# Chunked attention and a multiplicative feed-forward: another order of steps, with 100 zero products at its head

## The chip, the cores and the metric

The kernel runs on one core of one Trainium2 chip. The time is the device time of one execution in microseconds (us). A core has five engines that run side by side, each with its own queue in order: TensorE (PE, matrix products), VectorE (DVE), ScalarE (ACT), GpSimd (POOL) and SyncE (SP). PE writes its products to PSUM, a small memory of 8 banks; the other engines take them from there. POOL and SP also start DMA transfers, which 16 DMA engines carry out. An engine waits for another by semaphores.

## The reference

Attention within chunks of 64 positions, then a feed-forward whose two branches are multiplied:

```python
B, H, S, D = 8, 8, 576, 64;  chunk = 64
scores = scale * np.matmul(q_c, k_c.transpose(0, 1, 2, 4, 3))
attn = softmax(scores)                      # over the 64 positions of the chunk
x = np.matmul(attn, v_c)                    # gathered to (4608 tokens, 512)
a = x @ w1;  b = x @ w2                     # 512 -> 1024 each
out = ((a * b) @ w3) @ w_out                # 1024 -> 1024 -> 512
```

q, k, v and the weights are float32 in device memory. The kernel works in bfloat16 with float32 sums, and multiplies w3 by w_out once ahead (w3o), so the last two products are one.

## The kernel before, in words

The 72 chunks are worked in 18 *pairs* p = 0 to 17, each of 4 chunks (256 tokens). Every piece of work is a *step* with a letter and a pair, and the text `ORDER` (lines 9 to 40) lists all steps in the order in which they are issued. Nothing is planned at run time: each engine works its own share of that list in order. The letters:

- `q`, `k`, `v`: loads of a pair, started by POOL; `i0` to `i3`: quarters of w1 and w2; `o`: w_out; `h0`, `h1`: halves of w3. `R0`, `R1`: raw loads of pair 0's q and k on SP and ACT, which `K` casts. At most 8 of POOL's loads are under way: each waits for the landing of the eighth before it. There are 5 buffers for q and k (a pair each) and 6 for v.
- `T p.s`: DVE transposes q or k (line 205; 1.3 us). `G`: from pair 6 on, 8 moves on SP bring two pairs' transposed q and k into a form with fewer matmuls (line 216). `S`: scores on PE (line 226: 64 matmuls for pairs 0 to 5, 32 for later ones); `E`: exponential on ACT; `P`: product with v on PE (again 64 or 32 matmuls).
- `N p.u`: DVE divides by the sums (lines 266, 269); `X`: DVE transposes the result for the feed-forward; `H`: moves of it on SP for pairs from 6 on.
- `A`, `B`: products with w1 and w2 on PE (line 344); pairs 0 to 3 alone with 256 columns, later ones in twos with 512. `C`: ACT copies A's product from PSUM (line 367); `M`: DVE multiplies it by B's (line 384).
- `V`, `W`, `Z`: w3 times w_out: 8 transposes on DVE (line 425), 4 groups of 16 matmuls, 4 casts on ACT. V0 to V3 need `h0`, V4 to V7 `h1`; the two halves of a W need one V each.
- `O`: the last product (16 matmuls of 512 columns), `Y`: ACT copies it out of PSUM, `Q`: SP stores it.
- `D which.p.j.n.cols`: n matmuls of a zero tile into a PSUM tile, cols wide; their result is overwritten (lines 323 to 329).
- `x p`: POOL copies one element of pair p's attention result, so that the loads behind it wait for that (line 164).

PSUM holds 4 tiles of 2 banks. The lines that matter below: a matmul is always issued through one helper (line 96), as a weight load and a product, so each is two instructions of PE's program. That program is one straight list of 5,323 instructions.

Of the kernel before, what the change touches and what calls it, by code (L numbers as in the profile page):

```python
# [7 lines left out]

ORDER = """
R0 R1 v0 q1 k1 i0 v1 i1 i2 q2 k2 v2 i3 q3 k3 v3 q4 k4 v4 o h0 h1 D0.0.0.16.64 K0 T0.0 K1 T0.1 q5 k5  # L10
v5 S0 T1.0 E0 P0 D0.1.0.4.512 T1.1 q6 k6 v6 N0.0 S1 D1.0.0.5.512 X0.0 N0.1 X0.1 A0.0 E1 B0.0 C0.0 P1
M0.0 A0.1 N1.0 X1.0 B0.1 C0.1 N1.1 A0.2 X1.1 B0.2 M0.1 C0.2 A1.0 A1.1 B1.0 T2.0 T2.1 q7 B1.1 S2 M0.2
C1.0 C1.1 A0.3 E2 M1.0 P2 k7 B0.3 M1.1 A1.2 N2.0 C0.3 A1.3 B1.2 N2.1 X2.0 T3.0 C1.2 B1.3 X2.1 T3.1
C1.3 A2.0 M0.3 C2.0 B2.0 M1.2 q8 S3 A2.1 M1.3 A2.2 M2.0 E3 P3 T4.0 C2.1 C2.2 B2.1 N3.0 B2.2 N3.1
A2.3 B2.3 X3.0 X3.1 A3.0 M2.1 C2.3 M2.2 k8 A3.1 M2.3 B3.0 B3.1 T4.1 C3.0 q9 M3.0 C3.1 M3.1 A3.2 v7
V0 B3.2 C3.2 V1 A3.3 M3.2 S4 B3.3 W0 k9 C3.3 V2 V3 W1 Z0 V4 V5 T5.0 V6 V7 W2 Z1 W3 M3.3 T5.1 q10
T6.0 E4 T6.1 Z2 P4 T7.0 S5 T7.1 N4.0 Z3 k10 O0 T8.0 O1 q11 E5 N4.1 X4.0 Y0 G3.0 q12 X4.1 Y1 k11 P5
v8 N5.0 N5.1 O2 Q0 X5.0 X5.1 G3.1 A4.0 O3 T8.1 C4.0 Y2 S6 E6 S7 T9.0 T9.1 Q1 B4.0 T10.0 M4.0 A4.1
G4.0 T10.1 E7 P6 Y3 B4.1 v9 N6.0 C4.1 N6.1 A4.2 G4.1 C4.2 B4.2 M4.1 X6.0 M4.2 A4.3 P7 q13 q14 N7.0
Q2 B4.3 C4.3 A4.4 N7.1 k12 B4.4 M4.3 A4.5 X6.1 C4.4 C4.5 B4.5 A4.6 k13 k14 C4.6 M4.4 A4.7 S8 T11.0  # L20
v10 B4.6 B4.7 M4.5 q15 X7.0 X7.1 M4.6 C4.7 S9 M4.7 E8 P8 N8.0 O4 E9 N8.1 Q3 P9 Y4 H3.0 O5 T11.1 X8.0
T12.0 H3.1 v11 T12.1 Y5 N9.0 T13.0 A6.0 G5.0 B6.0 N9.1 X8.1 C6.0 X9.0 A6.1 C6.1 B6.1 T13.1 A6.2 B6.2
X9.1 M6.0 G5.1 A6.3 C6.2 H4.0 H4.1 q16 M6.1 B6.3 A6.4 M6.2 B6.4 C6.3 S10 M6.3 v12 C6.4 G6.0 E10 A6.5
T14.0 T14.1 M6.4 C6.5 B6.5 A6.6 M6.5 C6.6 B6.6 A6.7 C6.7 P10 M6.6 S11 N10.0 B6.7 A8.0 B8.0 E11 Q4
G6.1 N10.1 C8.0 M6.7 M8.0 X10.0 X10.1 k15 P11 A8.1 A8.2 B8.1 N11.0 B8.2 k16 A8.3 C8.1 C8.2 N11.1
X11.0 B8.3 A8.4 M8.1 v13 B8.4 S12 C8.3 M8.2 S13 C8.4 H5.0 X11.1 M8.3 A8.5 E12 A8.6 C8.5 M8.4 B8.5
C8.6 T15.0 H5.1 B8.6 A8.7 B8.7 T15.1 M8.5 E13 P12 M8.6 A10.0 T16.0 B10.0 N12.0 C8.7 A10.1 N12.1 M8.7
P13 C10.0 v14 M10.0 C10.1 B10.1 N13.0 N13.1 A10.2 M10.1 X12.0 A10.3 B10.2 X12.1 C10.2 C10.3 q17
A10.4 M10.2 B10.3 x12 G7.0 B10.4 X13.0 G7.1 C10.4 A10.5 v15 k17 M10.3 X13.1 M10.4 x11 A10.6 S14 S15
T16.1 T17.0 T17.1 B10.5 C10.5 B10.6 C10.6 E14 O6 M10.5 Q5 M10.6 E15 P14 N14.0 N14.1 G8.0 Y6 X14.0 O7  # L30
Y7 P15 G8.1 A10.7 H6.0 B10.7 S16 C10.7 N15.0 E16 N15.1 X14.1 X15.0 v16 v17 S17 M10.7 O8 E17 H6.1 Q6
Y8 P16 A12.0 B12.0 N16.0 A12.1 C12.0 M12.0 P17 B12.1 C12.1 N16.1 A12.2 C12.2 X15.1 B12.2 N17.0 H7.0
A12.3 C12.3 Q7 N17.1 M12.1 B12.3 A12.4 B12.4 M12.2 C12.4 A12.5 B12.5 M12.3 C12.5 M12.4 A12.6 Q8
C12.6 A12.7 H7.1 B12.6 B12.7 O9 C12.7 Y9 M12.5 M12.6 A14.0 B14.0 C14.0 M12.7 M14.0 A14.1 C14.1 A14.2
B14.1 A14.3 X16.0 C14.2 Q9 B14.2 X16.1 O10 Y10 M14.1 X17.0 H8.0 B14.3 A14.4 Q10 C14.3 X17.1 A14.5
M14.2 B14.4 C14.4 O11 Y11 A14.6 C14.5 M14.3 M14.4 A14.7 H8.1 A16.0 C14.6 B14.5 B14.6 B14.7 M14.5
C14.7 M14.6 Q11 M14.7 B16.0 A16.1 A16.2 C16.0 A16.3 B16.1 M16.0 C16.1 M16.1 A16.4 C16.2 C16.3 B16.2
C16.4 M16.2 A16.5 B16.3 O12 Y12 M16.3 C16.5 B16.4 A16.6 O13 Y13 M16.4 A16.7 B16.5 M16.5 C16.6 C16.7
Q12 B16.6 O14 B16.7 M16.6 Q13 O15 Y14 Q14 Y15 Q15 M16.7 O16 Y16 Q16 O17
"""  # L40


# [543 lines left out]
```

## Time and profile before

| | |
|---|---|
| time, median of 3 runs (all) | 245.23 us (243.93, 245.23, 246.45) |
| the profiled execution | 243.69 us, its span 242.1 us |
| PE busy | 225.9 us; last matmul ends at 238.86 us |
| DVE, ACT, POOL busy | 153.3, 84.2, 83.7 us |
| DMA engines | 0.9 busy or more until about 150 us |
| queue q8 (instructions) | 21 packets of 16,384 bytes |

The landing times that are used below, from the trace (us): the two parts of i1 18.06 and 19.17, of i2 20.52 and 21.84; k2 25.19; v2 26.51; the first half of w3 until 49.21, the second until 54.58; q5 56.01, k5 57.46; q10 80.91, k10 84.67.

A line of the timeline gives start, duration, engine, source line, operation, result and inputs, how many of them; in brackets the idle time of the engine ahead of it and what ended it ("issue": nothing that the profile shows). A line of the waits gives who waited for whom, us in total, how often, the longest. A line of the chain gives start, length and what it was.

### The profile page before, as it was taken

How to read it: one execution, taken by the hardware profiler on the slowest of the kernel's cores; microseconds unless marked ns; L12 is line 12 of the kernel's file. 1: busy time of each engine (PE TensorE's matmuls, PEld its weight loads, DVE VectorE, ACT ScalarE, POOL GpSimd, SP SyncE). 2: the span in 40 equal slices, each digit the busy share in tenths (PEclk: the TensorE clock that was granted, in tenths of full speed). 3: DMA queues.
4: the chain of work that ended last, by engine and by line, in shares of the span. 5: the costliest groups of instructions: out<-in, count | busy, mean ns of one | idle time of the engine just before them, and what ended most of it. 6: DMA issues, size and time to landing. Idle time of an engine off the chain costs nothing.

```text
span 242.1 us, 6230 instructions
## 1 busy us (share of the span) xinstructions
PE 225.9 (93%) x2625; PEld 119.2 (49%) x2625; DVE 153.3 (63%) x235; ACT 84.2 (35%) x116; POOL 83.7 (35%) x114
## 2 busy tenths in 40 slices
PE   1299879999999999999999999999999999999994
PEld 1248668874454444444444444444444444444443
DVE  1757878899985799879788999664833423321200
ACT  2412414213341453342543435153224025323122
POOL 7847965655973144742840092000000000000000
PEclk9999999999999999999999999999999999999999
DMA  6999999999999999999999799748202132003244
GB/s 175 178 185 181 185 169 199 196 191 173 170 175 263 253 215 264 199 222 195 210 272 191 174 202 150 153 112 298 52 4 88 43 130 87 3 0 117 84 150 173
DMA packets 94367, 39.23 MB, mean 162 GB/s; under 512 B 75265, under 2 KB 86785, under 8 KB 94337
## 3 DMA queue, kind: packets, MB, share of 16 engines
q0 software_dynamic: 82592, 18.88, 83.9%
q1 hardware_dynamic: 10704, 19.41, 27.2%
q10 hardware_dynamic: 1040, 0.52, 0.8%
q8 instruction: 21, 0.34, 0.6%
q14 instruction: 10, 0.07, 0.1%
HBM read 38.80 MB, written 9.44 MB: 199 GB/s over the span
## 4 chain that ended last, share of the span: by engine, by line
PE 85%; DMA 7%; DVE 3%; ACT 2%; issue 2%; SPq 0%; DVEq 0%; ACTq 0%
PE ab_ps L96 46%; PE o_ps L96 25%; PE w_ps L96 6%; DMA xt<-xm 4%; PE z_ps L96 3%; PE pv L96 3%; PE s_ps L96 2%; DMA raw<-in_q_dram 2%; ACT e L238 1%; DVE qkT L205 1%; DVE xm L310 1%; DMA qkm<-qkT 1%; DVE xn L269 1%; DVE ab L384 1%; ACT qk L145 0%
## 5 line engine op out<-in xcount | busy, mean ns | idle before, releaser
L96 PE MATMUL ab_ps<-xt,w 128*128 128x512 bf16 (+1 forms) x688 | 127.7, 342 | 0.5 <-issue 0.3
L96 PEld LDWEIGHTS <-w 128*128 128x128 bf16 x704 | 67.1, 98 | 54.9 <-issue 1.6
L384 DVE TENSOR_TENSOR ab<-a_sb,ab_ps 128x512 bf16<-128x512 f32 x71 | 46.8, 675 | 47.2 <-PE ab_ps L96 42.9
L96 PE MATMUL o_ps<-w3o,ab 128*128 128x512 bf16 (+1 forms) x296 | 64.7, 373 | 0.2 <-DVE ab L384 0.2
L367 ACT COPY a_sb<-ab_ps 128x512 f32<-128x512 f32 x71 | 41.4, 588 | 67.1 <-PE ab_ps L96 62.6
L205 DVE STREAM_TRANSPOSE qkT<-qk 128x1024 bf16<-128x1024 bf16 x36 | 45.8, 1296 | 8.3 <-ACT qk L145 5.3
L96 PEld LDWEIGHTS <-ab 128*128 128x128 bf16 x296 | 28.5, 98 | 32.5 <-issue 0.2
L99 POOL DMA_DIRECT2D vbuf<-in_v_dram x40 | 33.8, 850 | 23.9 <-DMA qk<-in_q_dram 7.2
L414 ACT COPY o_sb<-o_ps 128x1024 f32<-128x1024 f32 x17 | 17.2, 1013 | 53.1 <-PE o_ps L96 46.9
L269 DVE TENSOR_TENSOR xn<-pv,rcs 128x512 bf16<-128x512 f32 x36 | 24.9, 691 | 1.3
L99 POOL DMA_DIRECT2D qk<-in_q_dram x23 | 18.1, 788 | 12.5 <-DMA qk<-in_k_dram 3.7
L99 POOL DMA_DIRECT2D qk<-in_k_dram x23 | 18.0, 785 | 6.5 <-DMA vbuf<-in_v_dram 2.5
L238 ACT ACTIVATE e<-s_ps 128x1024 bf16<-128x1024 f32 x16 | 16.1, 1025 | 8.8 <-PE s_ps L96 8.7
L310 DVE STREAM_TRANSPOSE xm<-xn 128x512 bf16<-128x512 bf16 x24 | 16.0, 691 | 0.1
L266 DVE RECIPROCAL rcs<-pv 128x8 f32<-128x8 f32 x36 | 6.9, 193 | 13.8 <-PE pv L96 13.8
L96 PE MATMUL w_ps<-wo,w3T 128*128 128x512 bf16 x64 | 14.0, 379 | 0.0
L96 PE MATMUL pv<-vbuf,e 64*32 64x65 bf16 (+1 forms) x768 | 9.7, 198 | 3.3 <-issue 2.2
L99 POOL DMA_DIRECT2D w<-in_moe_w_dram x16 | 11.1, 694 | 4.7 <-DMA vbuf<-in_v_dram 1.7
L96 PEld LDWEIGHTS <-e 64*32 64x32 bf16 (+1 forms) x768 | 7.4, 99 | 9.9 <-issue 6.5
L96 PEld LDWEIGHTS <-w3T 128*128 128x128 bf16 x64 | 6.3, 98 | 7.3
L425 DVE STREAM_TRANSPOSE w3T<-w 128x1024 bf16<-128x1024 bf16 x8 | 9.6, 1225 | 0.5 <-DMA w<-in_moe_w_dram 0.4
L288 POOL CROSS_LANE_REDUCE all_good<-good 128x1 f32<-128x1 f32 x1 | 0.4, 354 | 25.5 <-DVE both L286 25.5
(29 smaller groups left out, 51.5 us busy)
## 6 DMA issues: line engine op xcount, KB each, us to landing
out_dram<-o_sb SPq DMA_DIRECT2D x17, 512.0 KB, 3.1
qkm<-qkT SPq DMA_DIRECT2D x48, 128.0 KB, 6.7
vbuf<-in_v_dram POOLq DMA_DIRECT2D x32, 128.0 KB, 7.8
w<-in_moe_w_dram POOLq DMA_DIRECT2D x16, 256.0 KB, 9.7
xt<-xm SPq DMA_DIRECT2D x48, 64.0 KB, 3.5
qk<-in_q_dram POOLq DMA_DIRECT2D x11, 256.0 KB, 9.7
qk<-in_k_dram POOLq DMA_DIRECT2D x11, 256.0 KB, 10.6
wo<-in_moe_w_out_dram POOLq DMA_DIRECT2D x4, 256.0 KB, 7.4
```

The costliest lines, as they stand in the source:

```text
L96: return inorder(nc.tensor.matmul(*a, **kw))
L99: return inorder(nc.gpsimd.dma_start(dst, src))
L205: inorder(nc.vector.transpose(qkT_t[g][:, :, p % 2, s, heads(h)].rearrange("p e h (y t) -> p h t e y", t=2), qk_t[p][:, s, heads(h)].rearr ...
L238: inorder(nc.scalar.activation(e_t[p][:, :, heads(hh)], s_t[p][:].rearrange("p u (h q) -> p u h q", q=CH)[:, :, heads(hh)], Exp, scale=sca ...
L266: inorder(nc.vector.reciprocal(rc, pv[:, :, :, D:W]))
L269: inorder(nc.vector.tensor_mul(xn_t[p][:, u], pv[:, :, :, 0:D], rc.to_broadcast([P, 2, 4, D])))
L288: inorder(nc.gpsimd.tensor_reduce(all_good[:], good[:], axis=mybir.AxisListType.C, op=op.add))
L310: inorder(nc.vector.transpose(xm_t[g][:, u, :, m].rearrange("p o (c y) -> p c o y", y=BL), xn_t[p][:].rearrange("p u r m d -> p (u r) m d" ...
L367: first[p, j] = inorder(nc.scalar.copy(a_t[p, j][:], ps_t[p, j][:, 0, :]))
L384: inorder(nc.vector.tensor_mul(o, view(a_t.pop((p, j))[:]), view(ps_t.pop((p, j))[:, 1, :])))
L414: inorder(nc.scalar.copy(o_sb[:], ps_t.pop(p)[:]))
L425: inorder(nc.vector.transpose(w3T_t[f][:].rearrange("p k (f y) -> p f k y", y=BL), w3[:, NB * f:NB * (f + 1), :].rearrange("p f (k x) -> p ...
```

## The change

All steps up to `h1` (the first loads) stay as they are. Behind them the same steps stand in another order. Within each letter the sequence of pairs stays, but for the `x` steps (x12 now stands ahead of the load of k17, behind v15, and x11 behind all loads). The zero products change: before there were 16 of 64 columns ahead of S0, 4 of 512 behind P0 and 5 of 512 behind S1; now there are 92 of 16 and 8 of 512 ahead of S0, and 5 of 512 behind S1. No other line of the file differs. Head of the list, and the places that the prediction speaks of:

```diff
-R0 R1 v0 q1 k1 i0 v1 i1 i2 q2 k2 v2 i3 q3 k3 v3 q4 k4 v4 o h0 h1 D0.0.0.16.64 K0 T0.0 K1 T0.1 q5 k5
-v5 S0 T1.0 E0 P0 D0.1.0.4.512 T1.1 q6 k6 v6 N0.0 S1 D1.0.0.5.512 X0.0 N0.1 X0.1 A0.0 E1 B0.0 C0.0 P1
-M0.0 A0.1 N1.0 X1.0 B0.1 C0.1 N1.1 A0.2 X1.1 B0.2 M0.1 C0.2 A1.0 A1.1 B1.0 T2.0 T2.1 q7 B1.1 S2 M0.2
-C1.0 C1.1 A0.3 E2 M1.0 P2 k7 B0.3 M1.1 A1.2 N2.0 C0.3 A1.3 B1.2 N2.1 X2.0 T3.0 C1.2 B1.3 X2.1 T3.1
...
-V0 B3.2 C3.2 V1 A3.3 M3.2 S4 B3.3 W0 k9 C3.3 V2 V3 W1 Z0 V4 V5 T5.0 V6 V7 W2 Z1 W3 M3.3 T5.1 q10
-T6.0 E4 T6.1 Z2 P4 T7.0 S5 T7.1 N4.0 Z3 k10 O0 T8.0 O1 q11 E5 N4.1 X4.0 Y0 G3.0 q12 X4.1 Y1 k11 P5
+R0 R1 v0 q1 k1 i0 v1 i1 i2 q2 k2 v2 i3 q3 k3 v3 q4 k4 v4 o h0 h1 D0.0.0.92.16 D0.0.0.8.512 K0 K1
+T0.0 T0.1 S0 E0 T1.0 P0 T1.1 N0.0 S1 N0.1 X0.0 D1.0.0.5.512 X0.1 A0.0 E1 B0.0 C0.0 P1 A0.1 M0.0 N1.0
+B0.1 C0.1 N1.1 A0.2 X1.0 X1.1 T2.0 C0.2 B0.2 A1.0 T2.1 M0.1 B1.0 S2 A1.1 B1.1 C1.0 M0.2 E2 P2 M1.0
+A0.3 C1.1 B0.3 N2.0 C0.3 q5 A1.2 N2.1 A1.3 B1.2 B1.3 T3.0 X2.0 X2.1 C1.2 M1.1 M0.3 q6 A2.0 B2.0 T3.1
...
+C2.2 k5 k6 C2.3 M2.1 M2.2 M2.3 q7 B3.0 C3.0 T4.1 A3.1 q8 A3.2 C3.1 k7 S4 M3.0 B3.1 V0 q9 k8 V1 M3.1
+V2 V3 E4 B3.2 W0 V4 Z0 T5.0 W1 Z1 V5 V6 C3.2 T5.1 W2 q10 V7 A3.3 W3 C3.3 T6.0 T6.1 Z2 B3.3 Z3 M3.2
+S5 P4 M3.3 T7.0 O0 T7.1 v5 N4.0 v6 O1 k9 N4.1 E5 Y0 P5 T8.0 X4.0 q11 G3.0 T8.1 X4.1 O2 G3.1 N5.0
+X5.0 k10 O3 Y1 S6 N5.1 T9.0 E6 Q0 Q1 X5.1 A4.0 T9.1 B4.0 Y2 k11 T10.0 T10.1 C4.0 A4.1 B4.1 G4.0
+T11.0 C4.1 M4.0 M4.1 A4.2 P6 N6.0 S7 N6.1 B4.2 A4.3 Y3 B4.3 v7 A4.4 C4.2 X6.0 B4.4 M4.2 E7 A4.5 C4.3
```

PE's program grows by 162 instructions (80 matmuls and two waits) to 5,485.

More of the change, by code (lines that the diff above doesn't have):

```diff
@@ L9 @@
 ORDER = """
-R0 R1 v0 q1 k1 i0 v1 i1 i2 q2 k2 v2 i3 q3 k3 v3 q4 k4 v4 o h0 h1 D0.0.0.16.64 K0 T0.0 K1 T0.1 q5 k5
-v5 S0 T1.0 E0 P0 D0.1.0.4.512 T1.1 q6 k6 v6 N0.0 S1 D1.0.0.5.512 X0.0 N0.1 X0.1 A0.0 E1 B0.0 C0.0 P1
-M0.0 A0.1 N1.0 X1.0 B0.1 C0.1 N1.1 A0.2 X1.1 B0.2 M0.1 C0.2 A1.0 A1.1 B1.0 T2.0 T2.1 q7 B1.1 S2 M0.2
-C1.0 C1.1 A0.3 E2 M1.0 P2 k7 B0.3 M1.1 A1.2 N2.0 C0.3 A1.3 B1.2 N2.1 X2.0 T3.0 C1.2 B1.3 X2.1 T3.1
-C1.3 A2.0 M0.3 C2.0 B2.0 M1.2 q8 S3 A2.1 M1.3 A2.2 M2.0 E3 P3 T4.0 C2.1 C2.2 B2.1 N3.0 B2.2 N3.1
@@ L15 @@
-A2.3 B2.3 X3.0 X3.1 A3.0 M2.1 C2.3 M2.2 k8 A3.1 M2.3 B3.0 B3.1 T4.1 C3.0 q9 M3.0 C3.1 M3.1 A3.2 v7
-V0 B3.2 C3.2 V1 A3.3 M3.2 S4 B3.3 W0 k9 C3.3 V2 V3 W1 Z0 V4 V5 T5.0 V6 V7 W2 Z1 W3 M3.3 T5.1 q10
-T6.0 E4 T6.1 Z2 P4 T7.0 S5 T7.1 N4.0 Z3 k10 O0 T8.0 O1 q11 E5 N4.1 X4.0 Y0 G3.0 q12 X4.1 Y1 k11 P5
-v8 N5.0 N5.1 O2 Q0 X5.0 X5.1 G3.1 A4.0 O3 T8.1 C4.0 Y2 S6 E6 S7 T9.0 T9.1 Q1 B4.0 T10.0 M4.0 A4.1
-G4.0 T10.1 E7 P6 Y3 B4.1 v9 N6.0 C4.1 N6.1 A4.2 G4.1 C4.2 B4.2 M4.1 X6.0 M4.2 A4.3 P7 q13 q14 N7.0
-Q2 B4.3 C4.3 A4.4 N7.1 k12 B4.4 M4.3 A4.5 X6.1 C4.4 C4.5 B4.5 A4.6 k13 k14 C4.6 M4.4 A4.7 S8 T11.0
@@ L21 @@
[L21 to L39, printed above, removed]
+R0 R1 v0 q1 k1 i0 v1 i1 i2 q2 k2 v2 i3 q3 k3 v3 q4 k4 v4 o h0 h1 D0.0.0.92.16 D0.0.0.8.512 K0 K1
+T0.0 T0.1 S0 E0 T1.0 P0 T1.1 N0.0 S1 N0.1 X0.0 D1.0.0.5.512 X0.1 A0.0 E1 B0.0 C0.0 P1 A0.1 M0.0 N1.0
@@ new lines @@
+B0.1 C0.1 N1.1 A0.2 X1.0 X1.1 T2.0 C0.2 B0.2 A1.0 T2.1 M0.1 B1.0 S2 A1.1 B1.1 C1.0 M0.2 E2 P2 M1.0
+A0.3 C1.1 B0.3 N2.0 C0.3 q5 A1.2 N2.1 A1.3 B1.2 B1.3 T3.0 X2.0 X2.1 C1.2 M1.1 M0.3 q6 A2.0 B2.0 T3.1
+C1.3 C2.0 S3 M1.2 A2.1 E3 A2.2 M1.3 M2.0 P3 C2.1 T4.0 N3.0 X3.0 B2.1 N3.1 B2.2 A2.3 X3.1 B2.3 A3.0
+C2.2 k5 k6 C2.3 M2.1 M2.2 M2.3 q7 B3.0 C3.0 T4.1 A3.1 q8 A3.2 C3.1 k7 S4 M3.0 B3.1 V0 q9 k8 V1 M3.1
+V2 V3 E4 B3.2 W0 V4 Z0 T5.0 W1 Z1 V5 V6 C3.2 T5.1 W2 q10 V7 A3.3 W3 C3.3 T6.0 T6.1 Z2 B3.3 Z3 M3.2
@@ new lines @@
+S5 P4 M3.3 T7.0 O0 T7.1 v5 N4.0 v6 O1 k9 N4.1 E5 Y0 P5 T8.0 X4.0 q11 G3.0 T8.1 X4.1 O2 G3.1 N5.0
+X5.0 k10 O3 Y1 S6 N5.1 T9.0 E6 Q0 Q1 X5.1 A4.0 T9.1 B4.0 Y2 k11 T10.0 T10.1 C4.0 A4.1 B4.1 G4.0
+T11.0 C4.1 M4.0 M4.1 A4.2 P6 N6.0 S7 N6.1 B4.2 A4.3 Y3 B4.3 v7 A4.4 C4.2 X6.0 B4.4 M4.2 E7 A4.5 C4.3
+G4.1 q12 C4.4 X6.1 M4.3 M4.4 P7 N7.0 Q2 S8 N7.1 B4.5 A4.6 C4.5 E8 M4.5 A4.7 B4.6 C4.6 X7.0 C4.7 X7.1
+B4.7 Q3 M4.6 S9 k12 M4.7 T11.1 v8 E9 P8 O4 N8.0 Y4 N8.1 q13 H3.0 H3.1 T12.0 X8.0 v9 P9 O5 X8.1 A6.0
@@ new lines @@
+Y5 A6.1 B6.0 C6.0 C6.1 N9.0 G5.0 A6.2 N9.1 X9.0 T12.1 v10 X9.1 B6.1 T13.0 A6.3 M6.0 B6.2 G5.1 B6.3
+M6.1 v11 H4.0 A6.4 C6.2 k13 C6.3 H4.1 M6.2 q14 A6.5 T13.1 q15 B6.4 G6.0 T14.0 S10 C6.4 M6.3 B6.5 k14
+M6.4 A6.6 T14.1 E10 B6.6 A6.7 C6.5 C6.6 M6.5 M6.6 P10 q16 N10.0 S11 C6.7 B6.7 k15 E11 N10.1 M6.7 v12
+A8.0 P11 B8.0 X10.0 N11.0 G6.1 A8.1 C8.0 C8.1 M8.0 N11.1 B8.1 A8.2 B8.2 S12 S13 M8.1 C8.2 X10.1 M8.2
+E12 A8.3 X11.0 B8.3 A8.4 C8.3 B8.4 X11.1 A8.5 E13 q17 T15.0 H5.0 M8.3 v13 B8.5 k16 C8.4 M8.4 T15.1
@@ new lines @@
+C8.5 A8.6 C8.6 T16.0 M8.5 A8.7 B8.6 P12 C8.7 H5.1 M8.6 N12.0 B8.7 M8.7 A10.0 A10.1 T16.1 N12.1 Q4
+B10.0 B10.1 A10.2 C10.0 C10.1 M10.0 v14 B10.2 C10.2 A10.3 G7.0 X12.0 G7.1 v15 x12 M10.1 k17 P13
+M10.2 S14 N13.0 N13.1 B10.3 X12.1 A10.4 E14 O6 X13.0 A10.5 C10.3 T17.0 T17.1 H6.0 B10.4 B10.5 C10.4
+M10.3 A10.6 C10.5 X13.1 Y6 M10.4 M10.5 P14 H6.1 N14.0 S15 G8.0 C10.6 B10.6 G8.1 A10.7 E15 B10.7
+C10.7 N14.1 P15 M10.6 Q5 X14.0 A12.0 C12.0 M10.7 N15.0 A12.1 B12.0 O7 N15.1 M12.0 Q6 C12.1 Y7 X14.1
+Q7 B12.1 O8 X15.0 S16 S17 v16 Y8 E16 E17 A12.2 O9 A12.3 X15.1 Q8 B12.2 B12.3 C12.2 M12.1 A12.4 v17
@@ new lines @@
+M12.2 C12.3 Y9 P16 M12.3 N16.0 C12.4 B12.4 A12.5 M12.4 N16.1 P17 N17.0 B12.5 X16.0 A12.6 H7.0 H7.1
+B12.6 A12.7 C12.5 C12.6 M12.5 B12.7 A14.0 B14.0 X16.1 N17.1 C12.7 M12.6 A14.1 Q9 O10 C14.0 M12.7 Y10
+A14.2 M14.0 C14.1 B14.1 M14.1 A14.3 X17.0 H8.0 A14.4 C14.2 C14.3 B14.2 B14.3 C14.4 M14.2 A14.5 X17.1
+B14.4 B14.5 M14.3 A14.6 H8.1 A14.7 M14.4 O11 C14.5 C14.6 M14.5 Q10 B14.6 A16.0 C14.7 C16.0 M14.6 Y11
+B14.7 A16.1 C16.1 B16.0 M14.7 A16.2 B16.1 B16.2 A16.3 C16.2 M16.0 C16.3 O12 M16.1 B16.3 A16.4 M16.2
@@ L40 @@
+A16.5 B16.4 Y12 A16.6 B16.5 M16.3 C16.4 A16.7 Q11 x11 C16.5 M16.4 O13 Q12 B16.6 Y13 B16.7 C16.6
+C16.7 O14 Q13 M16.5 M16.6 M16.7 Y14 Q14 O15 Y15 Q15 O16 Y16 Q16 O17
 """
```

## The prediction, made before the changed kernel was run

> **What bounds the kernel now.** I read the page first, for the busy shares; then what TensorE (PE) waited for; then the chain that ended last; then the timeline up to 75 us; and last the packets of the instruction queue and the landing times of the loads.
>
> ```profile
> PE 225.9 (93%) x2625; PEld 119.2 (49%) x2625; DVE 153.3 (63%) x235; ACT 84.2 (35%) x116; POOL 83.7 (35%) x114
> ...
> q8 instruction: 21, 0.34, 0.6%
> ```
>
> ```profile
> PE z_ps L96 <- DVE qkT L205: 7.2, 1, 7.2
> PE pv L96 <- issue: 2.2, 1, 2.2
> PE z_ps L96 <- DVE zero L115: 1.4, 1, 1.4
> PE pv L96 <- ACT e L238: 1.1, 1, 1.1
> ```
>
> ```profile
> 66.43 0.63 PE pv L96 x64
> 67.06 0.64 PE s_ps L96 x64
> 67.69 7.01 PE o_ps L96 x32
> ...
> 193.07 3.45 PE ab_ps L96 x16
> ```
>
> PE is the bound and nearly all of its time is useful. The chain gives the prices: 16 matmuls of 512 columns 3.45 (0.2157 each), an early S or P 0.64 or 0.63, a late one 0.38; the matmuls of 256 columns start 0.109 apart. So the useful work is 448 x 0.2157 + 256 x 0.109 (A, B) + 288 x 0.2157 (O) + 64 x 0.2157 (W) + 6 x 1.27 + 12 x 0.76 (S, P) = 217.2 us. The last matmul ends at 238.86: 21.7 us are lost, 18.45 of them before 31.7 us and 0.5 more up to O0 at 67.69. What is lost later is some 0.1 us at each change of matmul kind, and there are as many of these in the new order (16 places with late S or P in both). A different order can therefore matter only in the first 70 us, unless it makes new waits.
>
> **Why P2 stood for 2.2 us.** The longest wait that is not the start has no data behind it:
>
> ```profile
> 29.00 0.53 PE L96 MATMUL pv<-vbuf,e 64*32 64x65 bf16 x45
> ...
> 31.68 0.27 PE L96 MATMUL pv<-vbuf,e 64*32 64x65 bf16 x19 [2.16 <-issue]
> ```
>
> v2 had landed at 26.5. Queue 8 carried 21 packets of 16,384 bytes, and PE's program has 5,323 instructions: 256 to a packet. PE stopped without a data wait at exactly two places, at its instructions 450 (17.7 to 18.25) and 963 (P2): two packets apart. The packets ran at 15.78 to 16.67 and 29.21 to 30.15; PE went on 1.58 and 1.53 us after their ends. So blocks of 256 begin at instructions 194, 450, 706 and so on, and block k+1 is asked for when PE's sequencer enters block k. From entry to packet it took 4.06, 4.43, 3.98, 3.79, 3.64, 4.30, 4.08 and 4.76 us for eight blocks between 18 and 84 us, while loads fill the DMA engines; 2.3 to 2.5 after 180 us, where they are idle. Entry to use is then 4.0 + 0.95 + 1.55 = 6.5 us. An early S with its P is 256 instructions in 1.3 us, so where both stand in one block, PE can outrun its program. The sequencer is up to 64 instructions ahead of PE, but a semaphore wait holds it: blocks 1, 7, 11 and 12 were asked for 5.1 to 7.4 us after a free sequencer would have been there, and about 4 us (block 11: 2.2) after the step that waited had started.
>
> The Trainium skill, "Runtime: NRT & Kernel Launch", section "Instruction fetch mechanics", has the same blocks (16 KiB, 256 instructions) but says that crossing one is "mostly hidden". Here two crossings cost 0.5 and 2.2 us. By the page's rule the stall forecast below would not be there; that is the first rival.
>
> **The change part by part** (new times by the rows of before).
> *Zeros.* 16 of 64 columns, 4 and 5 of 512 go; 92 of 16, then 8 and 5 of 512 come: 80 matmuls, 160 instructions more. The trace has no 16-column row. Nearest is the 64-column one, 0.053 apart; scaled by columns it is 0.013. The 512-column zeros started 0.427 apart cold and 0.216 once the matmuls had sped up at 16.6. So the first hundred end between 1.44 + 92 x 0.013 + 8 x 0.216 = 4.4 and 1.44 + 92 x 0.053 + 8 x 0.427 = 9.7. S0 cannot start before the transpose of k0 at 9.6, so they cost 0 to 0.2 us (I take 0). If they leave PE fast, S0 takes 0.65 and not 1.07; but N0.0 (12.36) follows T1.1 on VectorE, which ends at 12.39, and so does not move. What moves is A0.0: x is ready at about 15.5 in both (its last transpose ended at 15.6), and in before the cold zeros held PE until 17.1. A0.0 gains 1.6.
> *Up to W0.* P1 then starts at 17.4 and meets block 3 (asked for at P0, as block 2 was in before; ready at 18.2): its end is 18.5, not 20.06. A0.1 to B0.2 wait for the same weight loads (landing 18.06, 19.17, 20.52, 21.84). S2 now stands before A1.1, B1.1 and A0.3 and needs T2.1: k2 lands at 25.19, so S2 is at 26.6 to 27.3 after 2 us of idling. A1.1, B1.1, P2 (29.2 to 29.9) and A0.3 follow; PE is 1.3 ahead. Block 6 is ready at 40.0, 0.6 after P3 needs it; P3 ends at 40.5 against 41.2. S4, B3.1 and B3.2 end at 49.85. W0 needs V0, and V0 the first half of w3, which lands at 49.21 in both, since all loads up to h1 keep their order:
>
> ```profile
> 49.34 2.37 DVE L425 STREAM_TRANSPOSE w3T<-w 128x1024 bf16<-128x1024 bf16 x2 [0.16 <-DMA w<-in_moe_w_dram]
> ...
> 52.45 7.72 PE L96 MATMUL w_ps<-wo,w3T 128*128 128x512 bf16 x35
> ...
> 54.80 2.55 DVE L425 STREAM_TRANSPOSE w3T<-w 128x1024 bf16<-128x1024 bf16 x2 [0.24 <-DMA w<-in_moe_w_dram]
> ```
>
> W0 starts at 50.6 with 1.7 us less work done before it. The front's gain is down to 0.15, and 0.75 us of slack stands before W0, so small errors above do not count.
> *W to O0.* On VectorE, V4 waits for w3's second half (54.58, as before): V4, T5.0 (q5 landing 56.0), V5, V6, T5.1 and V7 end at 62.35. PE runs W0 to W2, A3.3, W3 (to 65.3), B3.3, S5, P4. B3.3 ends at 66.2 against 66.36 for the same work. Then the new order puts S5 and P4 into one block: block 8 begins 6 matmuls before the end of W3, block 9 after 50 of P4's 64. Block 8's first instruction stands behind the wait for V7, so block 9 is asked for at 62.35 and usable at 62.35 + 6.5 = 68.85. P4 reaches it at 67.4: **1.45 us of stall** (1.1 to 2.2 with delays of 3.64 to 4.76). In before this boundary lay in P5, behind 7.0 us of O0 and O1. O0 starts at 69.0, not 67.69: +1.3.
> *Behind O0.* PE is later by 1.3, and the loads and moves nearly keep their clock. q and k come earlier, v5 to v7 later: v5 lands about 71 (P5 at 76), v6 about 74 (P6 at 88), v7 about 89 (P7 at 94). v8 and v9 keep about 1 us. The POOL copy that held v15 for 14.8 us now stands behind it; P15 was never near. Blocks 10 to 21 each hold over 7 us of work. I take 0 here.
> Sum: 242.1 + 1.3 = 243.4 us of span, and 243.69 + 1.3 = 245.0 for this execution. The median of the runs shown (245.23) is 1.5 above that execution; the forecast for the median is 245.23 + 1.3 = **246.5**.
>
> **The clock gate.** The granted clock is 1.00 in every window, yet matmuls of 512 columns ran at half rate until 16.6. The Trainium skill, "TensorE: Matmul & The Clock Gate", section "What you observe", describes a PE that speeds up after some 4 us of steady work. By that rule zeros up to S0 save 0.4 us at S0 and some 1.5 by A0.0. The rows say the same of A0.0, but also that W0 gives it back.
>
> **Rivals.**
> 1. *No stall in P4*: a sequencer that V7's wait does not hold asks for block 9 at 57.5 and has it in time; O0 at 67.55, change -0.15: 245.1. Against it: the two stalls of before, and blocks 1, 7, 11, 12. Chance 0.20. (It is also what the Trainium skill's page above would lead to.)
> 2. *Clearly slower: the second group of k and q moves (G4) ends late for S8.* S8 stands 2.6 us of PE work earlier. G4 starts when T9.1 ends, 82.3 (81.7 before); its last move landed 12.0 after its first issue, so now at 94.3, and S8 is due at 74.2 + 20.3 = 94.5 (in before 2.4 us were left). T9.1 needs k9 by 81.0; from there on its delay goes straight into the span. By load order k9 should land about 76, but in before loads came up to 4.6 us apart (86.13 to 90.71) once moves shared the engines. If k9 lands where before's k10 did (84.67), S8 slips by 3.7: 250.2. Chance 0.24.
> 3. *Faster: the front's gain lives on.* If w3's halves landed 1.5 us sooner, W0 could start at 49.85 and V7 end sooner; with the stall gone too, some -1.5: 243.7. The same queue in the same order speaks against it. Chance 0.08.
> 4. *The zeros do not speed PE up*: A0.0 at 15.9 and not 15.5, inside the slack before W0; the time of the forecast, and part of its chance.
> The forecast has 0.48.
>
> **Numbers.** 1% (2.45 us) is about what a measurement here can tell from no change. The forecast's own range is +0.9 to +2.0. Range: rival 3 at the low end, 243.8; most of rival 2 at the high end, 249.8. Faster by over 1%: 0.05 (the tail of rival 3); slower: 0.27 (rival 2 and a little of the forecast with another stall); within 1%: 0.68.
>
> **What would show it.** After: 22 packets on queue 8; A0.0 near 15.5; W0 near 50.6 behind w3's load; a wait of PE in pv put down to issue of about 1.5 near 67.4; O0 near 69.0; everything behind it with before's distances plus 1.3. Wrong if P4 runs through, if W0 starts before 50, or if S8, P8 or P9 wait for a DMA.

## The result and the profile after

The changed kernel takes 247.31 us in the median of 20 runs (246.09 to 250.58); the kernel before takes 244.96 in 20 runs beside it (243.69 to 246.90). The ratio is 1.0081, with a 95% interval of 1.0054 to 1.0107: a little slower, and within the 1% that was forecast as the likeliest class. The forecast was 246.5, by a stall of 1.45 us in P4 that makes O0 1.3 us later. That stall does not exist; the time is lost elsewhere. The ratios of this document leave out runs over 1.5% above the fastest of their kernel; among the kernels below this matters for tail_alone, where it takes out 5 of 12, the profiled one (253.59) among them.

The page of the changed kernel, the lines that answer to those of before, and the shares of the chain that ended last:

```profile
PE 230.7 (94%) x2686; PEld 123.6 (50%) x2705; DVE 152.8 (62%) x235; ACT 84.1 (34%) x116; POOL 83.8 (34%) x114
...
q8 instruction: 21, 0.34, 0.6%
...
PE 46%; DMA 42%; POOL 5%; issue 3%; DVE 2%; SPq 1%; DVEq 0%; POOLq 0%
```

In before PE made up 85% of that chain and DMA 7%. Now DMA is 42% of it. PE's busy time grew by 4.8 us, of which 3.1 are the zeros (7.9 after 4.8). PE's waits (who for whom, total, how often, longest):

```profile
PE ab_ps L96 <- DMA qkm<-qkT: 1.3, 1, 1.3
...
PE s_ps L96 <- DMA qkm<-qkT: 1.2, 1, 1.2
...
PE w_ps L96 <- DVE w3T L425: 1.0, 1, 1.0
PE pv L96 <- DVE ab L384: 0.5, 1, 0.5
```

The wait of 2.2 us "issue" in P2 is gone; four waits of PE for moves or for VectorE stand in its place. The timeline of PE shows where (start, length, in brackets the idle time ahead), the changed kernel first, then the products of before that answer to its last two:

```profile
28.95 0.70 PE L96 MATMUL pv<-vbuf,e 64*32 64x65 bf16 x64
...
50.46 7.73 PE L96 MATMUL w_ps<-wo,w3T 128*128 128x512 bf16 x34 [1.01 <-DVE w3T L425]
...
66.76 0.70 PE L96 MATMUL pv<-vbuf,e 64*32 64x65 bf16 x64
67.39 7.08 PE L96 MATMUL o_ps<-w3o,ab 128*128 128x512 bf16 x31
...
87.69 0.45 PE L96 MATMUL pv<-vbuf,e 64*64 64x65 bf16 x32 [0.48 <-DVE ab L384]
...
109.41 9.66 PE L96 MATMUL ab_ps<-xt,w 128*128 128x512 bf16 x44 [1.28 <-DMA qkm<-qkT]
...
131.66 0.93 PE L96 MATMUL s_ps<-qkm 64*64 64x64 bf16 x63 [1.22 <-DMA qkm<-qkT]
```

```profile
107.10 5.12 PE L96 MATMUL ab_ps<-xt,w 128*128 128x512 bf16 x23 [0.26 <-issue]
...
131.37 0.71 PE L96 MATMUL s_ps<-qkm 64*64 64x64 bf16 x64
```

P2 (28.95) and P4 (66.76) run through. O0 starts at 67.39, against 67.62 in before (the 67.69 of before's chain is a later matmul of O0). To compare the two orders I take each step's start and subtract the useful work that PE's list has ahead of it, by the prices of the prediction. What is left is PE's loss up to that step:

| loss of PE up to (us) | before | after |
|---|---|---|
| O0 | 18.87 | 18.64 |
| P7 | 19.27 | 20.14 |
| O4 | 19.64 | 20.93 |
| A6.0 | 20.17 | 22.48 |
| S12 and S13 (the first product behind its wait) | 20.4 | 24.3 |
| O17, the last | 21.41 | 25.43 |

Behind O0 the changed order loses 6.8 us where before loses 2.5. Three places make 3.7 of the 4.3 us between them: P6 and S7 (1.0), A6.0 (1.0) and S12 (1.65, of which 1.22 are the wait shown). The chain from 74 to 132 us names what was late (start, length, what):

```profile
74.89 19.40 DMA vbuf<-in_v_dram
...
102.98 6.08 DMA xt<-xm
109.08 7.68 DMA qkm<-qkT
116.77 5.87 DMA xt<-xm
122.66 8.87 DMA qkm<-qkT
131.66 0.93 PE s_ps L96 x63
```

The first line is v7, loaded behind k11 in the new list: issued at 74.89, landed at 94.29. The second half of P7 (93.95 to 94.65) needs it, X7 follows, then the moves of H3, whose last lands at 109.06, and A6.0. The "qkm<-qkT" that the wait line names at A6.0 is a piece that ended at nearly the same time; A6.0 reads what H3 moves. The last DMA is the last move of G6, which S12 reads. From H3's last move on, the chain is one move of SP after another up to S12: by it the third wait hangs on the second, and the three places are not independent.

The pair of profiles differs by 4.0 us (247.71 and 243.69), the medians by 2.35. Why, is shown below: the profile of before is not its typical run.

### The profile page after: what moved, and what is told of

It reads as the page before. It is cut to its first block, busy times and chain, and to the rows that moved or that the text cites. A ratio compares the mean times of both kernels' runs of the same rounds, so it can differ in the third digit from the quotient of the medians.

```text
span 246.2 us, 6372 instructions
## 1 busy us (share of the span) xinstructions
PE 230.7 (94%) x2686; PEld 123.6 (50%) x2705; DVE 152.8 (62%) x235; ACT 84.1 (34%) x116; POOL 83.8 (34%) x114
## 4 chain that ended last, share of the span: by engine, by line
PE 46%; DMA 42%; POOL 5%; issue 3%; DVE 2%; SPq 1%; DVEq 0%; POOLq 0%
PE ab_ps L96 27%; PE o_ps L96 17%; DMA vbuf<-in_v_dram 15%; DMA qkm<-qkT 8%; DMA w<-in_moe_w_dram 7%; DMA xt<-xm 5%; DMA qk<-in_q_dram 4%; DMA qk<-in_k_dram 3%; POOL vbuf L99 2%; SPq L197 1%; POOL qk L99 1%; PE s_ps L96 1%; PE pv L96 1%; DVE w3T L425 1%; POOL wo L99 1%
## 5 line engine op out<-in xcount | busy, mean ns | idle before, releaser
L96 PEld LDWEIGHTS <-w 128*128 128x128 bf16 x704 | 67.9, 99 | 56.4 <-DMA qkm<-qkT 1.9
L96 PE MATMUL o_ps<-w3o,ab 128*128 128x512 bf16 (+1 forms) x284 | 63.7, 373 | 0.6
L238 ACT ACTIVATE e<-s_ps 128x1024 bf16<-128x1024 f32 x17 | 17.3, 1025 | 23.8 <-PE s_ps L96 23.8
L96 PE MATMUL z_ps<-zero 128*128 128x16 bf16 (+1 forms) x103 | 7.9, 223 | 1.9 <-DVE zero L115 1.4
```

The source lines that it names most:

```text
L96: return inorder(nc.tensor.matmul(*a, **kw))
L238: inorder(nc.scalar.activation(e_t[p][:, :, heads(hh)], s_t[p][:].rearrange("p u (h q) -> p u h q", q=CH)[:, :, heads(hh)], Exp, scale=sca ...
```

## The experiments

Each kernel is timed against before on the same chip; ratios are to it, with 95% intervals.

### 1 to 4: zeros, head, tail and loads apart

`zeros_alone` is before with the new zeros. `head_alone` has the new order on every engine up to O0 and the old one behind it; `tail_alone` is the reverse. `loads_before` is the changed kernel with POOL's list of before.

```diff
 zeros_alone, in the list of before
-... h0 h1 D0.0.0.16.64 K0 T0.0 ... P0 D0.1.0.4.512 T1.1 ...
+... h0 h1 D0.0.0.92.16 D0.0.0.8.512 K0 T0.0 ... P0 T1.1 ...
 loads_before, POOL's share of the list of after, behind h1
-q5 q6 k5 k6 q7 q8 k7 q9 k8 q10 v5 v6 k9 q11 k10 k11 v7 q12 k12 v8 ...
+q5 k5 v5 q6 k6 v6 q7 k7 q8 k8 q9 v7 k9 q10 k10 q11 q12 k11 v8 v9 ...
```

> The steps stay in the order of before; only the zero products are those of the changed kernel (92 of 16 and 8 of 512 columns ahead of S0, 5 of 512 behind S1, the 4 of 512 behind P0 gone). Theory A (the time comes from the order behind O0, where PE meets the moves of q, k and x; the zeros only move the block boundaries of PE's program by 162 instructions): the boundary that stood in P2 now stands in the middle of S2 and is needed only 27.5 - 20 = 7.5 us after the block ahead of it was entered, so P2's 2.2 us go; W0 is then held by w3's first half at 50.5 and not 52.45, O0 starts at 65.7 and not 67.6, and the kernel takes 243.0 to 244.6. Theory B (the zeros or the moved boundaries are what made the changed kernel slower): 246 to 248. Theory C (the order of the loads): within 0.5 of before.

> The changed kernel's order on every engine up to O0, and behind it each engine's remaining steps in the order of before. Theory A: O0 at 67.4 (0.2 us earlier than in before), no PE wait over 0.5 us between 82 and 132 us but that of A6.0, time 244.3 to 245.3. Theory B (zeros, blocks): O0 or what follows is late, 246.5 to 248. Theory C (the order of the loads; q5 to q10 and k5 to k8 are loaded in the new order, v5 and v6 behind them): half of the loss, 246.

> The order and the zeros of before on every engine up to O0, and behind it each engine's remaining steps in the order of the changed kernel. Theory A: O0 at 67.6, then the three losses of the changed kernel: about 1.0 us at P6 and S7, 1.0 at A6.0 and 1.5 at S12, time 246.8 to 248. Theory B: as before, 244.5 to 245.5. Theory C: half of the loss, 246.

> The changed kernel, with POOL's list (all loads and the two copies that hold some of them) in the order of before. Theory A: the order on PE against the moves on SP decides, so A6.0 and S12 still wait for moves and the time is 246.3 to 248; only the 1.0 us at P6 may go, where VectorE stands in a transpose that waits for k10. Theory C (the order of the loads): no such waits, 244.5 to 245.5.

| | median (us) | ratio | O0 in its profile |
|---|---|---|---|
| zeros_alone | 244.41 | 0.9973 (0.9941 to 1.0005) | 66.00 |
| head_alone | 244.44 | 0.9966 (0.9934 to 0.9997) | 67.40 |
| tail_alone | 250.57 (all 12) | 1.0127 (1.0077 to 1.0176) | 67.77 |
| loads_before | 251.29 | 1.0254 (1.0198 to 1.0311) | 67.99 |

Against before, neither the zeros nor the new head cost anything, so the loss comes with the new tail. Theory B falls. tail_alone is slower too, but not as theory A had it: it keeps before's order of loads up to q11, with v7 early, and its profile shows 6.2 us of waiting at P6, no more than 0.2 at A6.0 and 0.6 at S12, where about 1.0, 1.0 and 1.5 were expected. The zeros alone even bring O0 forward by 1.6 us, since P2's stall is gone, but all of it is gone again by the end: behind O0 PE loses 5.6 us in this profile and 2.5 in that of before. PE's waits of zeros_alone:

```profile
PE ab_ps L96 <- DMA xt<-xm: 1.0, 1, 1.0
PE ab_ps L96 <- DMA qkm<-qkT: 0.7, 1, 0.7
PE pv L96 <- DVE ab L384: 0.7, 1, 0.7
```

From 80 to 125 us loads and moves share the DMA engines, and a PE that comes earlier meets them sooner; that this is why these waits came is read from the trace and was not tested.

With loads_before both theories missed: the old order of loads made the new tail worse. VectorE's and PE's timeline of that run:

```profile
89.28 1.31 DVE L205 STREAM_TRANSPOSE qkT<-qk 128x1024 bf16<-128x1024 bf16 x1 [3.35 <-DMA qk<-in_q_dram]
90.50 1.24 DVE L384 TENSOR_TENSOR ab<-a_sb,ab_ps 128x512 bf16<-128x512 f32 x2
...
91.19 0.45 PE L96 MATMUL pv<-vbuf,e 64*64 64x65 bf16 x32 [3.08 <-DVE ab L384]
```

The new tail has T10.0, T10.1 and T11.0 ahead of M4.0 on VectorE; before has only T10.0 there. T11.0 waits for q11 (here 89.2), M4.0 and M4.1 stand behind it, and P6 has no free PSUM tiles until M4.0 is done. In the changed kernel the same place costs 0.5 because there q11 had landed by 79.4 and only k10 was late (84.6); in the profile of tail_alone, where q11 came at 91.5, it cost 6.2. These two waits cost more than their length: behind them the granted clock was 0.50 for 3.4 us (from 91.8) in loads_before and for 6.8 us (from 92.5) in tail_alone. This is the first of the three places: a product held in a queue behind a transpose whose load is late.

### 5 to 8: the three places, one by one

```diff
 m4_before_t, VectorE
-T9.1 T10.0 T10.1 T11.0 M4.0 M4.1 N6.0 N6.1 X6.0 M4.2 X6.1 M4.3 M4.4 N7.0
+T9.1 M4.0 T10.0 M4.1 N6.0 N6.1 X6.0 M4.2 T10.1 X6.1 M4.3 M4.4 T11.0 N7.0
 m4_and_v7, in addition: POOL, PE (E7, N7, X7 go with P7; T11.0 stands behind X7.1)
-k9 q11 k10 k11 v7 q12          P6 S7 B4.2 A4.3 B4.3 A4.4 B4.4 A4.5 P7 S8
+k9 v7 q11 k10 k11 q12          P6 S7 B4.2 A4.3 P7 B4.3 A4.4 B4.4 A4.5 S8
 s12_late, PE (E12, E13 go with them)
-B8.2 S12 S13 A8.3 B8.3 A8.4 B8.4 A8.5
+B8.2 A8.3 B8.3 A8.4 B8.4 S12 S13 A8.5
 three_undone: all of these
```

> The changed kernel; on VectorE, M4.0 stands ahead of T10.0, T10.1 behind M4.2 and T11.0 behind M4.4, so that no product that PE waits for stands behind a transpose whose load (k10, q11) is late. Theory A1 (each of the three late places costs by itself): PE's wait of 0.5 at P6 and 0.15 at S7 go, time 0.9 below the changed kernel, ratio to before 1.004. Theory A2 (the loads and moves keep a clock of their own): the wait goes, but P7 still follows v7's landing and A6.0 still waits for H3's moves, so at A6.0 nothing is left of it; ratio 1.007 to 1.009.

> As the run before; and v7 is loaded ahead of q11 (in the changed kernel it stands behind k11 and lands at 94.3), P7 stands behind A4.3 as in before, with its exponential, N7 and X7 as far forward, so H3's moves are issued earlier. Theory A2: A6.0 waits for H3 no more (1.3 us) and nothing at P6, so some 2 us are won at A6.0; S12 then waits for G6 longer than the 1.2 of the changed kernel by what of these 2 us G6 does not follow; ratio 1.001 to 1.005. If the loads' order does not matter: A6.0 waits as before this edit, 1.007 to 1.009.

> The changed kernel; on PE, S12 and S13 stand behind B8.4 (as in before) and not behind B8.2: 3.45 us of products later; their exponentials behind C8.4 and C8.5. Theory A1 and A2: the wait of 1.2 us for G6's moves at S12 goes and nothing behind it waits in its place; 1.2 to 1.5 below the changed kernel, ratio to before 1.002 to 1.004. Rival: the moves of H5 and G7 and the last loads set the pace there, and P12, A10.0 or S14 wait instead; 1.007 to 1.009.

> The changed kernel with all three edits: M4 ahead of the late transposes, v7 and P7 early, S12 and S13 behind B8.4. Theory: no wait of PE over 0.5 us between 70 and 140 us, time 244.3 to 245.3 (ratio 0.995 to 1.000), as the new head with the old tail gave. If another cause takes part in the loss (the loads of q5 to q10 ahead of v5 and v6, the places of the stores), 246 or more.

| | median | ratio |
|---|---|---|
| m4_before_t | 248.25 | 1.0122 (1.0073 to 1.0172) |
| m4_and_v7 | 246.21 | 1.0040 (1.0008 to 1.0073) |
| s12_late | 246.48 | 1.0049 (1.0012 to 1.0087) |
| three_undone | 248.77 | 1.0101 (1.0040 to 1.0161) |

m4_before_t: theory A2 holds, though its ratio lies above the 1.007 to 1.009 of the forecast, which its interval still takes in. The wait at P6 went (0.47 is left at S7), and nothing was won; PE now stands for v7 inside P7 and again at A6.0:

```profile
94.55 0.32 PE L96 MATMUL pv<-vbuf,e 64*64 64x65 bf16 x16 [0.71 <-DMA vbuf<-in_v_dram]
...
109.90 2.32 PE L96 MATMUL ab_ps<-xt,w 128*128 128x512 bf16 x10 [1.52 <-DMA qkm<-qkT]
```

m4_and_v7: with v7 loaded ahead of q11, and P7 and X7 earlier by it, the wait at A6.0 is gone, and the ratio falls from 1.0122 to 1.0040. So the late v7 with the late P7 is the cause of the second loss; what the load's place is worth without P7's was not tried. S12 was expected to wait longer than 1.2 here; it waited 0.22, though neither it nor G6 was moved. So most of the third wait goes with the second, as the chain above has it:

```profile
130.07 0.93 PE L96 MATMUL s_ps<-qkm 64*64 64x64 bf16 x63 [0.22 <-DMA qkm<-qkT]
```

s12_late: the wait at S12 is gone and the kernel is faster than the changed one, but less so than forecast; part of it comes back 15 us later. three_undone missed its forecast of 244.3 to 245.3 by 4 us. In its profile O0 comes 0.95 later than in the changed kernel (68.34), with W0 at 51.41, which no edit touched. Its S12 does not wait, but S14 does:

```profile
147.13 0.19 PE L96 MATMUL s_ps<-qkm 64*64 64x64 bf16 x1
149.85 0.67 PE L96 MATMUL s_ps<-qkm 64*64 64x64 bf16 x31 [2.53 <-DMA qkm<-qkT]
```

S14 needs the last move of G7. In this run it was issued at 144.81 and landed at 149.72; in m4_and_v7 142.18 and 144.60. Between the two lies the load of k17, v16 and v17, which the copy x12 (ahead of k17 in the new order) lets go at 144.1 here and at 143.4 there. In s12_late, where S14 waited 0.8, it was 142.72 to 146.98, with k17 let go at 143.1. The last move took 2.4 us where it was issued 1.3 us ahead of k17's load, 4.3 where it was 0.4 ahead and 4.9 where it was 0.7 behind. That the loads, and so the x step, are to blame was not tested by moving it. So the three places are where the changed kernel waits, but they do not add up: undoing all three leaves it as slow as it was.

### 9 and 10: the stall that was forecast, and the clock

`late_v7` is the changed kernel with `T6.0 T6.1 V7` in place of `V7 T6.0 T6.1` on VectorE. `before_again` is before, unchanged. ("35 of 52" in the expectation for it should read 33.)

> The changed kernel; on VectorE, V7 stands behind T6.0 and T6.1, so it ends near 64.2 and not at 61.7; the second half of W3 then waits 0.8, and P4 reaches the block boundary at 67.9 to 68.0. If a semaphore wait holds PE's sequencer (the reason of the forecast stall): the packet that was taken at 63.47 in the changed kernel moves by the same 2.5 us or more, to 66.0 (1.8 behind V7's end, as there) up to 68.2 (4.0 behind it), is usable 2.45 later at 68.4 to 70.6, and P4 stands for 0.5 to 2.7 us. If the sequencer runs ahead of the wait: the packet stays within 0.5 of 63.5 and P4 runs through.

> The kernel before, unchanged, for a second profile of it. In 35 of 52 of its later runs the mean granted clock was 0.990 to 0.993 and the span some 2 us longer than in the rest, whose clock was 0.997 to 1.00 (the profile of before is one of the latter, with 1.00). Theory D: the clock is halved for some 4 us behind PE's stall in P2 (27 to 36 us), so B0.3 and what follows up to S3 run slow, and O0 starts near 69.5 and not at 67.6; span 244 to 245. Rival: the clock is lowered between 80 and 100 us, where PE waits for products and moves, or before 20 us, where it costs nothing. If this run has the clock of 1.00, nothing is learned.

late_v7 (VectorE, then PE; its time 246.72, one run):

```profile
62.65 1.18 DVE L425 STREAM_TRANSPOSE w3T<-w 128x1024 bf16<-128x1024 bf16 x1
...
63.89 1.90 PE L96 MATMUL w_ps<-wo,w3T 128*128 128x512 bf16 x8 [0.52 <-DVE w3T L425]
...
67.23 0.70 PE L96 MATMUL pv<-vbuf,e 64*32 64x65 bf16 x64
```

V7 ended at 63.83 and the second half of W3 waited for it. The packet of the next block, asked for by an instruction behind that wait, ran from 63.06: before V7 was done, and not 2.5 us later than in the changed kernel (63.47) but 0.4 earlier. So this wait does not hold PE's sequencer, and P4 ran through. In this run and in that of the changed kernel the packet came some 5 us after a sequencer 64 instructions ahead of PE could have been there.

before_again took 245.91, its span was 244.4 and its mean clock 0.991. PE's windows of 2 us (columns: window, its length and PE's busy time with the number of matmuls, granted clock, DMA share, GB/s), then its timeline:

```profile
28.00:30.00 2.00, 1.62 (x68) 1.00 1.80 187
30.00:32.00 2.00, 0.28 (x19) 0.92 2.20 162
32.00:34.00 2.00, 2.00 (x21) 0.50 1.96 173
34.00:36.00 2.00, 2.00 (x15) 0.73 2.03 178
36.00:38.00 2.00, 2.00 (x21) 1.00 1.89 173
```

```profile
31.73 0.35 PE L96 MATMUL pv<-vbuf,e 64*32 64x65 bf16 x19 [1.94 <-issue]
32.01 7.77 PE L96 MATMUL ab_ps<-xt,w 128*128 128x256 bf16 x56
```

Theory D holds in this run: behind P2's stall the granted clock is halved for some 3.4 us, the same 56 matmuls take 7.77 us where they took 6.29 in the first profile of before, and O0 starts at 69.23 instead of 67.62. The line of the first profile:

```profile
31.88 6.29 PE L96 MATMUL ab_ps<-xt,w 128*128 128x256 bf16 x56
```

Of 86 later runs of before, 48 had a mean clock of 0.986 to 0.993 and a median of 246.1; the other 38, at 0.997 or more, 243.95. The changed kernel has no stall there. Its 13 runs at 0.978 to 0.986 have a median of 246.99, its 5 at 0.998 or more 247.53: no cost (the other two, at 0.991 and 0.993, took 250.6 and 249.1). In the profiles of zeros_alone and m4_before_t, with such clocks, the low clock lay between 9.5 and 19.7 us, ahead of the waits for k and w3, which can take up what is lost there. So before carries a loss of its own in more than half of its runs, which the change removes, and that is why the medians are nearer than the profiles. (That the stall brings the low clock on is read from its place, and from tail_alone: it has before's head, and none of its runs has a clock above 0.993.) zeros_alone and head_alone, level with before in the table, are some 0.5 us slower than its runs without that loss.

### 11 and 12: a faster version, and the number of zeros

`best1` is zeros_alone with VectorE's list put right where PE's waits came from; `best2` is best1 with other zeros of about the same length.

```diff
 best1, VectorE, against before (PE: S8, with E8, behind B4.6 and not ahead of it)
-T9.1 T10.0 M4.0 T10.1 N6.0 N6.1 M4.1 X6.0 M4.2 N7.0 N7.1 M4.3 X6.1 M4.4 T11.0 M4.5 X7.0 X7.1 M4.6 M4.7
+T9.1 M4.0 T10.0 N6.0 N6.1 M4.1 X6.0 M4.2 N7.0 N7.1 M4.3 X6.1 X7.0 X7.1 M4.4 M4.5 T10.1 M4.6 T11.0 M4.7
-T12.0 T12.1 N9.0 T13.0 N9.1 X8.1 X9.0 T13.1 X9.1 M6.0
+T12.0 N9.0 N9.1 X8.1 X9.0 X9.1 T12.1 M6.0 T13.0 T13.1
 best2, against best1
-D0.0.0.92.16
+D0.0.0.57.48
```

> The order of before with the zeros of the changed kernel (O0 at 66.0 in that run), and VectorE's list put right where PE's waits came from: M4.0 ahead of T10.0; T10.1 and T11.0 as late as M4.5 and M4.6; X7.0 and X7.1 directly behind N7.1, M4.3 and X6.1, so H3's moves start near 92.5 instead of 95.6; N9, X8.1 and X9 ahead of T12.1, which waits for k12, so H4's moves start near 107 instead of 111.9; S8 one product later. Theory: PE's waits at P6 (0.7), A6.0 (1.0) and A8.0 (0.7) go and 1.5 to 2.5 us of the span with them: 242 to 243, ratio to before 0.984 to 0.991. If the loads and moves keep their clock whatever VectorE's order is: the waits come back at S10, S12 or S14, and the time is 244 to 245.

> The run before (best1) with 57 zero products of 48 columns where it has 92 of 16: 35 products, 70 instructions fewer, of about the same length together. In best1 PE stood for 1.0 us in the products behind P2 (34.3) with no data to wait for, 1.5 us behind the end of an instruction packet (31.87 to 32.80). If the block boundaries explain it: that boundary moves 35 products back, to 64 products (7 us) behind P2, where its packet is long there; the wait at 34.3 goes, O0 starts 0.8 to 1.2 us earlier than in best1 (66.88), down to the floor that w3's load sets (W0 near 50.6, O0 near 65.8), and the time is 242.3 to 242.9, or 243.2 again if the moves behind O0 take the gain back. If that wait has another cause, it stays at 34.3 and O0 at 66.9.

best1 takes 243.19 us, ratio 0.9928 (0.9899 to 0.9958): faster than both kernels. The waits at P6 and A6.0 are gone, and A8.0 waits no more; PE's loss behind O0 is 3.0 us, against 5.6 in zeros_alone. Against the runs of before without the low clock (244.1 in the same series) it gains 0.9 us. It is a little over the forecast, for one because O0 came at 66.88, 0.9 us later than in zeros_alone, half of it here:

```profile
34.31 3.12 PE L96 MATMUL ab_ps<-xt,w 128*128 128x256 bf16 x27 [0.99 <-issue]
```

best2 takes 247.50, ratio 1.0108 (1.0070 to 1.0146). The wait at 34.3 went as forecast, but two others came:

```profile
15.92 0.69 PE L96 MATMUL s_ps<-qkT 32*64 32x64 bf16 x34 [2.77 <-issue]
...
31.92 6.29 PE L96 MATMUL ab_ps<-xt,w 128*128 128x256 bf16 x56
...
43.22 0.23 PE L96 MATMUL pv<-vbuf,e 64*32 64x65 bf16 x9 [1.99 <-issue]
```

PE went on 1.58 and 1.30 us behind the end of a packet (13.45 to 14.34, and 40.95 to 41.92). Boundaries now lie in S1 and P3, and there PE outran its program. The first of these packets was asked for too late: with 70 instructions fewer ahead of S0, the block in front of it begins some 64 instructions behind S0's start, which is as far as the sequencer gets while PE waits for k0 (S0 started at 9.66, the packet 3.79 later); in best1 the packet that answers to it came at 8.06. Between these two kernels nothing differs but a row of products whose result is overwritten, and 4.3 us hang on it.

## Why the prediction was right, and where it was wrong

- *What bounds the kernel*: right that PE is the bound. Wrong that an order can matter only in the first 70 us. The text itself named the exception, new waits, and they came between 87 and 132 us.
- *Blocks of 256 instructions, 6.5 us from entry to use*: the blocks and their places hold (P2 without stall in the changed kernel, the stalls of best2). There are 21 packets, not 22.
- *Zeros*: they cost nothing at S0 (9.93 against 9.64; the last ended at 7.5, inside the range). 16 columns took 0.028 us each, between the two bounds. They did not speed PE up in this run: S0 took 1.07, and A0.0 came at 16.59 and not at 15.5. That is rival 4, and as it said it does not matter, because of the next step. "The granted clock is 1.00 in every window" was misread: the trace of before has no record of the clock ahead of 16.8 us, that of the changed kernel none ahead of 19.3, and a window without one reads 1.00. The half rate up to these times fits a low clock: A0.0's 16 products took 3.24 us here, 0.2 each against 0.109.
- *W0 at 50.6 behind w3's first half, the front's gain down to 0.15*: right. W0 started at 50.46 after 1.01 of waiting, and O0 came 0.23 earlier.
- *P4's stall of 1.45, O0 at 69.0*: **the step that failed.** "A semaphore wait holds it" was read from four blocks of before, and V7's wait holds nothing (late_v7). The packet was in time: rival 1, with a chance of 0.20. Why the four blocks of before were asked for late stays open. By the prediction's own sign ("Wrong if P4 runs through") its mechanism failed. The Trainium skill, "Runtime: NRT & Kernel Launch", section "Instruction fetch mechanics", calls a crossing "mostly hidden". P4 agrees, P2 of before (2.2) and best2 (2.8 and 2.0) do not: by these rows it is hidden only where PE needs the next block some 6.5 us or more after its sequencer entered the one before.
- *Behind O0: 0.* **The second step that failed**, and the one that set the time: +4.2 in the profiles. The text checked when q, k and v land for P5 to P7, S8 and P8, and found each in time; v7, taken at 89, landed at 94.29. It did not follow P7 on to X7, H3 and A6.0, nor look what stands behind T10.1 in VectorE's list, nor compare S12's new place (3.45 us of products earlier) with G6.
- *Rival 2* had the right kind of cause, moves and loads on shared DMA engines, at the wrong place: k9 landed at 75.9 and G4 at 92.7, in time for S8 (94.5).
- The forecast's time, 246.5, lies only 0.8 below what was measured, and that is luck, because two errors cancel: a stall of 1.3 that did not come, some 3.4 us at full clock behind O0 (243.95 to 247.3) that did, and less of it in the medians because before's own clock loss goes.

## What to carry over

In a kernel whose order is a list, follow each moved load through every step that hangs on it to the next product on the bound engine, and look at what stands behind each waiting instruction in its queue. Here a gain ahead of a stage that is paced by DMA was given back in it (zeros_alone); repair the waits in that stage first (best1), and expect the next chain of moves to show up where one is shortened (three_undone). And compare a profile's clock with that of the timed runs before taking its time as the kernel's.

## What was not expected of the hardware

- A stall of PE of only 1.9 us was followed by some 3.4 us at half the granted clock; more than half of before's runs have a mean clock like that run's. The Trainium skill, "TensorE: Matmul & The Clock Gate", section "What's actually happening", puts the return to the slow state after an idle window of about 3.4 us; here less was enough.
- After the hundred zeros, S0 took 0.71 us in five profiled runs of the new zeros and 1.02 to 1.07 in five, with PE idle ahead of it for 2.2 to 2.5 us in the former and 2.3 to 3.3 in the latter; in best2 it took 0.71 after 3.9. The idle time does not tell them apart, but the record of the granted clock does. Where S0 took 0.71, a stretch at 1.00 was running when it began (zeros_alone 6.99 to 10.40, S0 9.61 to 10.32). Where it took longer, that stretch had ended or was about to (three_undone 9.22, S0 from 10.05; loads_before 9.90, S0 from 9.80), or the record begins only behind S0 (the changed kernel 19.31, m4_and_v7 18.95). Why it begins so late in these two stays open. The stretches at 0.50 within the kernels last 3.41, 6.83 or 10.24 us, one, two or three times the same length.
- In the changed kernel a load of q or k issued between 45 and 60 us landed 8 to 10 us later; v7, issued at 74.9 while SP's moves ran beside it, took 19.4 (and q10 to k11 of before 14 to 21).
